# A list schedule in place of a hand-written order of the work, and another sharing of the PSUM banks

## The chip, the core and the metric

The kernel runs on one core of a Trainium2 chip. TensorE (PE) multiplies, VectorE (DVE) and ScalarE (ACT) move and transform tiles, GpSimd (POOL) builds masks and issues the DMAs that cast fp32 to bf16, SyncE (SP) issues the other DMAs. Each engine takes its instructions strictly in the order in which the program emits them; semaphores hold an instruction until its inputs are there. The metric is the device time of one execution in microseconds (us).

## The reference

For each of 4 batches the kernel computes an attention of 8 heads over 768 positions with head size 64, and feeds the result to a mixture of experts. The attention is sparse: a query sees the keys less than 16 positions away, and beside them 24 block keys (the maximum over each block of 32 keys) whose values are block means.

```python
scores_l = scale * q @ k.T                      # kept where |i - j| < 16
scores_s = scale * q @ k_blockmax.T + log(32)   # 24 block keys
a = softmax(concat([masked scores_l, scores_s]))
x = a @ concat([v, v_blockmean])                # 4 x 768 x (8*64 = 512)
e = argmax(x.mean(axis=1) @ w_gate)             # one expert of 8 per batch
out = gate_prob * (relu(x @ w1[e]) @ w2[e])     # 512 -> 1024 -> 512
```

The expert of a batch is known only when the whole attention of that batch is done; only then can its two weight matrices (2 MB each in fp32) be fetched.

## The kernel before, in words

A batch b has an attention part and an expert part (MoE). The attention part works on four pairs of heads (pr 0 to 3), each in two halves of the sequence (hf 0 and 1), with these steps:

- T(pr): TensorE transposes K into the PSUM tile kps (line 229) and Q into tps (250); K is evacuated into windows of 96 keys (244 on ScalarE in batch 0, 246 on VectorE later), Q on VectorE (256), the block maxima are taken (260) and copied beside the windows (266).
- QK(pr, hf): 12 small matmuls into sc (280), exponential (289), mask (290).
- AV(pr, hf): 12 small matmuls into one PSUM bank (316), reciprocal and scaling (324, 325).
- X(pr): transposes back (337), evacuated into xT with the sum for the gate (342).

The values of a batch are loaded in 8 DMAs, one per head, on SP's queue (`load_v`, 97). They are cast to bf16 (`cast_v`, 186 on VectorE, 184 on ScalarE), the 16 rows before and behind each block are copied by DMA (`halo_v`, 191 and 192), the block means are made on TensorE (`vsum`, 200), evacuated (209) and spread by DMA (213). `load_qk` (92) issues the loads of K and Q from POOL's queue. `gate` (395 to 441) forms the logits, finds the expert, issues the loads of w1 and w2 on POOL's queue (417, 422) and makes the scale of the output. The MoE part (`moe_groups`) has 16 groups h (451, evacuated at 458) and 6 groups o (465, evacuated at 473, stored from SP's queue at 474).

The order is written by hand. Batch 0's attention runs first, as a list of steps (line 379). From then on the MoE groups of batch b and the steps of batch b+1's attention (line 386) alternate in proportion to their number (lines 516 to 526); `LEAD` steps of batch 1 come ahead. Within a step the instructions are emitted together.

The eight PSUM banks: kps 1, tps 1, sc 2, ops 1 (AV of batches 1 to 3), mps 3 (MoE groups, the block means, the gate, and AV of batch 0).

Of the kernel before, what the change touches and what calls it, by code (L numbers as in the profile page):

```python
# [18 lines left out]
AX = mybir.AxisListType  # L19


@with_exitstack
def kernel(
# [10 lines left out]
    nc = tc.nc  # L34
# [28 lines left out]
    xt_pool = ctx.enter_context(tc.tile_pool(name="xt", bufs=2))  # L63
# [33 lines left out]
    def load_v(b):  # L97
        for h in range(H):
            if b > 0:
                nc.sync.dma_start(  # L100
                    v_f[16:80, :, h, :], v[b, h].rearrange("(j p) d -> p j d", p=QB)
                )
                continue
            j0 = 1 if h == 0 else 0
            nc.sync.dma_start(
                v_f[:, j0:NJ, h, :],
                bass.AP(
                    tensor=v.tensor,
                    offset=v.offset + (h * S + j0 * QB - 16) * D,
                    ap=[[D, 80], [QB * D, NJ - j0], [1, D]],  # L110
                ),
            )
            if h == 0:
                nc.sync.dma_start(v_f[16:80, 0, 0, :], v[0, 0, 0:QB, :])

    load_qk(0, 0, 2)
    nc.vector.memset(v_f[0:16, 0, 0, :], 0.0)
    load_v(0)
    wg_sb = const_pool.tile([128, NDT, E], FP32, name="wg_sb")
    nc.sync.dma_start(wg_sb, moe_w_gate.rearrange("(g p) e -> p g e", p=128))  # L120

    warm = const_pool.tile([1, 8], FP32, name="warm")
    nc.vector.memset(warm, 0.0)
    nc.scalar.activation(warm, warm, ACT.Exp)
    nc.vector.memset(kps.rearrange("p g c -> p (g c)").bitcast(FP32), 0.0)

    identb = const_pool.tile([128, 128], BF16, name="identb")
    make_identity(nc, identb)

# [3 lines left out]
    bind = const_pool.tile([80, NJ, 32], BF16, name="bind")  # L133
    nc.vector.memset(mask1, 1.0)
# [3 lines left out]
    def keep(t, pattern, base, mult):  # L138
# [10 lines left out]
    keep(mask1, [[-1, G], [-G, QB // G]], -1, 1)  # L149
    keep(mask1, [[1, G], [G, QB // G]], 31, -1)  # L150
    keep(row_in, [[0, 1]], 79, -1)
    keep(bind, [[QB, NJ], [-BLK, 32]], -16, 1)
    keep(bind, [[-QB, NJ], [BLK, 32]], 47, -1)
    keep(bind, [[0, NJ], [0, 32]], -16, 1)

    tok = const_pool.tile([80, 2], BF16, name="tok")
    nc.gpsimd.tensor_copy(tok[:, 0:1], v_f[:, NJ - 1, 3, 0:1])
    load_qk(0, 2, 4)
    nc.gpsimd.tensor_copy(tok[:, 1:2], v_f[:, NJ - 1, 6, 0:1])
    load_qk(0, 4, 6)  # L160
    load_qk(0, 6, 8)

    nc.vector.tensor_copy(mask[0:KW], mask1.unsqueeze(1).to_broadcast([KW, NJ, QB]))
    nc.vector.memset(mask[0:16, 0, :], 0.0)
    nc.vector.tensor_scalar(
        out=mask[0:KW, NJ - 1, :], in0=mask1, scalar1=row_in[:, 0:1], scalar2=None, op0=ALU.mult
    )
    nc.vector.memset(mask[KW:NR], 1.0)
    ones_row = const_pool.tile([1, 128], FP32, name="ones_row")
    nc.vector.memset(ones_row, 1.0)  # L170

    def init_vblk(i):
        nc.vector.memset(vblks[i][64:KW, NJ - 1, :, :], 0.0)
        nc.vector.memset(vblks[i][0:KW, :, :, D : D + 1], 1.0)

    init_vblk(0)
    for t in kts:
        nc.gpsimd.memset(t[:, :, NR:128], 0.0)

    def cast_v(b, h0, h1, eng):  # L180
        dst = vblks[b % 2][0:80, :, h0:h1, 0:D]
        src = v_f[:, :, h0:h1, :]
        if eng is nc.scalar:
            nc.scalar.activation(dst, src, ACT.Copy)
        else:
            eng.tensor_copy(dst, src)  # L186

    def halo_v(b, h0, h1):
        vb = vblks[b % 2]
        if b > 0:  # L190
            nc.sync.dma_start(vb[0:16, 1:NJ, h0:h1, :], vb[64:80, 0 : NJ - 1, h0:h1, :])
        nc.sync.dma_start(vb[80:96, 0 : NJ - 1, h0:h1, :], vb[16:32, 1:NJ, h0:h1, :])

    def vsum(b, groups):
        vb = vblks[b % 2]
        vs_ps = mps_pool.tile([128, 512], FP32, name="hps", tag="mps")
        HW = H // 2
        for j in range(NJ):
            for i, hg in enumerate(groups):
                nc.tensor.matmul(  # L200
                    vs_ps[32 * i : 32 * i + 32, 0 : HW * (D + 1)],
                    lhsT=bind[:, j, :],
                    rhs=vb[0:80, j, hg * HW : (hg + 1) * HW, :],
                    start=(j == 0),
                    stop=(j == NJ - 1),
                )
        n = 32 * len(groups)
        vsb = sm_pool.tile([64, HW, D + 1], BF16, name="vsb")
        nc.vector.tensor_copy(
            vsb[0:n], vs_ps[0:n, 0 : HW * (D + 1)].rearrange("p (h c) -> p h c", c=D + 1)  # L210
        )
        for i, hg in enumerate(groups):
            nc.sync.dma_start(
                vb[KW:NR, :, hg * HW : (hg + 1) * HW, :],
                vsb[32 * i : 32 * i + NB].unsqueeze(1).to_broadcast([NB, NJ, HW, D + 1]),
            )

    def attn_steps(b):
        q_nat, k_nat = qk_nat[b]
        vb = vblks[b % 2]  # L220
        xT = xt_pool.tile([128, NP, S], BF16, name="xT_b")
# [136 lines left out]
        def halo():  # L358
            if nxt < B:
                halo_v(nxt, 0, H)  # L360
# [196 lines left out]
```

## Time and profile before

| | us |
|---|---|
| median of 3 runs (lowest, highest) | 258.3 (257.16, 259.15) |
| the profiled execution | 257.47 |
| its span, from the first to the last instruction | 255.9 |
| PE busy in the span | 160.2 |
| DVE busy | 99.1 |
| ACT busy | 97.2 |
| POOL busy | 25.5 |

A busy share is a mean over stretches that have different limits: an engine with 63% can be the limit in one stretch and starved in another. So the span is read in stretches, and in each the wait is looked for that ended last.

### The profile page before, as it was taken

The numbers are of one execution on the slowest core, as the hardware profiler recorded it, in microseconds if no ns is written. First come the engines' busy times: TensorE is split into PE (matmuls) and PEld (weight loads), VectorE is DVE, ScalarE is ACT, GpSimd is POOL, SyncE is SP. The second block draws the span as 40 slices with busy tenths as digits, with TensorE's granted clock in tenths as the row PEclk, the third lists the DMA queues.
The fourth block names the chain that finished last, engine by engine and source line by source line (L and its number), as shares of the span: only waits on it lengthen the run. The fifth ranks groups of instructions, "written<-read, shape, count | busy, mean of one in ns | idle before, by whom it ended". The sixth has DMA issues, their size and how long they took to land. (4 is left out here: it accounts for less than half of the span.)

```text
span 255.9 us, 4606 instructions
## 1 busy us (share of the span) xinstructions
PE 160.2 (63%) x1936; PEld 95.8 (37%) x1960; DVE 99.1 (39%) x201; ACT 97.2 (38%) x183; POOL 25.5 (10%) x46
## 2 busy tenths in 40 slices
PE   0205457731254889967550498964989897539993
PEld 0203346510143655544230355442555454115541
DVE  4204337753047785237450255524464623100000
ACT  2211546620013449632300567532348555105542
POOL 7260000009000000005000000002000000200000
PEclk9999999999999999999795599999599999657998
DMA  7999209708999980469999400446950023495033
GB/s 119 191 185 179 44 14 167 108 1 124 181 207 208 208 125 4 98 148 180 198 196 204 152 3 3 106 138 103 218 120 3 0 85 124 69 207 96 0 123 123
DMA packets 46869, 30.45 MB, mean 119 GB/s; under 512 B 28224, under 2 KB 42144, under 8 KB 46752
## 3 DMA queue, kind: packets, MB, share of 16 engines
q0 software_dynamic: 13264, 14.68, 35.9%
q1 hardware_dynamic: 33584, 15.47, 29.8%
q8 instruction: 15, 0.25, 0.4%
q14 instruction: 6, 0.05, 0.1%
HBM read 36.06 MB, written 6.29 MB: 166 GB/s over the span
## 5 line engine op out<-in xcount | busy, mean ns | idle before, releaser
L451 PE MATMUL hps<-xT_b,w_sb 128*128 128x256 bf16 (+1 forms) x245 | 51.8, 348 | 22.6 <-ACT o_sb L473 12.6
L465 PE MATMUL hps<-w_sb,hT_sb 128*128 128x512 bf16 x179 | 46.5, 404 | 1.9 <-issue 1.2
L290 DVE TENSOR_TENSOR aT<-aT,mask 120x768 bf16<-120x768 bf16 x32 | 17.8, 558 | 64.5 <-ACT aT L289 64.4
L451 PEld LDWEIGHTS <-w_sb 128*128 128x128 bf16 x256 | 24.2, 104 | 39.5 <-issue 20.9
L458 ACT ACTIVATE hT_sb<-hps 128x512 bf16<-128x512 f32 x64 | 29.3, 497 | 16.8 <-PE hps L451 16.8
L473 ACT ACTIVATE o_sb<-hps,gcol 128x512 f32<-128x512 f32 x24 | 16.5, 686 | 44.2 <-PE hps L465 19.4
L289 ACT ACTIVATE aT<-sc 128x768 bf16<-128x768 f32 x32 | 25.9, 810 | 12.7 <-PE sc L280 12.7
L280 PE MATMUL sc<-qT,kT 64*128 64x64 bf16 x384 | 13.5, 212 | 25.3 <-ACT kT L266 9.4
L266 ACT ACTIVATE kT<-kmx 128x288 bf16<-128x288 bf16 x16 | 7.1, 442 | 56.3 <-DVE kmx L260 56.3
L465 PEld LDWEIGHTS <-hT_sb 128*128 128x128 bf16 x192 | 18.7, 102 | 22.0 <-issue 4.8
L200 PE MATMUL hps<-vblk,bind 80*32 80x260 bf16 x96 | 12.0, 347 | 18.1 <-DMA vblk<-vblk 9.0
L417 POOL DMA_DIRECT2D w_sb<-in_moe_w_dram x5 | 4.5, 911 | 186.7 <-DVE gcol L441 98.9
L280 PEld LDWEIGHTS <-kT 64*128 64x128 bf16 x384 | 9.7, 107 | 33.9 <-issue 14.3
L246 DVE COPY kT<-kps 128x1152 bf16<-128x1152 bf16 x12 | 16.2, 1352 | 4.1 <-PE kps L229 4.1
L200 PEld LDWEIGHTS <-bind 80*32 80x32 bf16 x96 | 7.6, 118 | 21.7 <-issue 18.5
L342 ACT ACTIVATE xT_b<-tps 128x768 bf16<-128x768 bf16 x16 | 13.0, 811 | 6.4 <-PE tps L337 6.3
L260 DVE TENSOR_REDUCE kmx<-kT 128x24 bf16<-128x768 bf16 x16 | 15.1, 943 | 0.0
L229 PE MATMUL kps<-identb,k_nat 96*64 96x96 bf16 x256 | 11.0, 245 | 6.4 <-DMA k_nat<-in_k_dram 6.4
L316 PEld LDWEIGHTS <-aT 120*64 120x64 bf16 x384 | 10.3, 127 | 9.9 <-issue 5.3
L325 DVE TENSOR_TENSOR xs<-ops,rv 128x384 bf16<-128x384 f32 x24 | 13.4, 557 | 0.8
L186 DVE CAST vblk<-v_f 80x1536 bf16<-80x1536 f32 (+1 forms) x13 | 13.4, 1042 | 0.5 <-DMA v_f<-in_v_dram 0.5
L337 PE MATMUL tps<-identb,xs 128*128 128x128 bf16 x96 | 10.3, 247 | 4.6 <-DVE xs L325 3.2
(57 smaller groups left out, 120.7 us busy)
## 6 DMA issues: line engine op xcount, KB each, us to landing
w_sb<-in_moe_w_dram POOLq DMA_DIRECT2D x7, 1024.0 KB, 13.6
out_dram<-o_sb SPq DMA_DIRECT2D x24, 256.0 KB, 2.1
v_f<-in_v_dram SPq DMA_DIRECT2D x24, 192.0 KB, 13.0
k_nat<-in_k_dram POOLq DMA_DIRECT2D x6, 384.0 KB, 18.5
q_nat<-in_q_dram POOLq DMA_DIRECT2D x6, 384.0 KB, 20.6
v_f<-in_v_dram SPq DMA_DIRECT2D x7, 240.0 KB, 7.8
vblk<-vsb SPq DMA_DIRECT2D x8, 146.2 KB
vblk<-vblk SPq DMA_DIRECT2D x6, 178.8 KB
```

Source lines behind the costliest of these rows:

```text
L186: eng.tensor_copy(dst, src)
L200: nc.tensor.matmul(vs_ps[32 * i : 32 * i + 32, 0 : HW * (D + 1)], lhsT=bind[:, j, :], rhs=vb[0:80, j, hg * HW : (hg + 1) * HW, :], start=( ...
L246: nc.vector.tensor_copy(kdst, win)
L260: nc.vector.tensor_reduce(out=kmx.rearrange("p (j n) -> p j n", n=2), in_=kT[:, :, 16:80].rearrange("p j (n w) -> p j n w", w=BLK), axis=AX.X,
L280: nc.tensor.matmul(sc[:, hh, jj * QB : (jj + 1) * QB], lhsT=kTs[pr][rs, j, :], rhs=qTs[pr][rs, j, :], start=True, stop=True, tile_position ...
L289: nc.scalar.activation(aT, sc[:, :, 0 : NH * QB], ACT.Exp, scale=SCALE)
L290: nc.vector.tensor_tensor(out=aT[0:NR], in0=aT[0:NR], in1=mask[:, hf * NH : (hf + 1) * NH, :] .rearrange("p j c -> p (j c)") .unsqueeze(1) ...
L325: nc.vector.tensor_tensor(out=xss[pr][:, hf * NS : (hf + 1) * NS, :, :].rearrange("p s h d -> p h s d"), in0=ops[:, :, :, 0:D], in1=rv.uns ...
L451: nc.tensor.matmul(hps[:, 0 : c1 - c0], lhsT=w1_sb[:, dt, ft * 128 : (ft + 1) * 128], rhs=xT_b[:, dt, c0:c1], start=(dt == 0), stop=(dt == ...
L458: nc.scalar.activation(hT[:, ft, c0:c1], hps[:, 0 : c1 - c0], ACT.Relu)
L465: nc.tensor.matmul(o_ps, lhsT=hT[:, ft, st * 128 : (st + 1) * 128], rhs=w2_sb[:, ft, :], start=(ft == 0), stop=(ft == NFT - 1),)
L473: nc.scalar.activation(o_sb, o_ps, ACT.Copy, scale=gcol[:, 0:1])
```

## The change

The emission order is no longer written out. Each step is cut into its parts (one TensorE group, one evacuation, one DMA issue), and each part is entered as an operation with its engine, a duration, its dependencies and, for a DMA, a transfer time. A list scheduler goes through the graph when the program is built: at each turn it takes the engine that can start first, and on it the operation with the longest remaining chain, or a shorter one that fits ahead of it; it emits that operation. The result is again one fixed order per engine.

```diff
+class Sched:
+    SEM = 0.06
+    URGENT = 3.0
...
+    def slot(self, tag, bufs):
+        q = self.tags.setdefault(tag, [])
+        q.append({"first": None, "readers": []})
+        deps = []
+        if len(q) > bufs:
+            deps += q[-1 - bufs]["readers"]
+        if len(q) > 1:
+            deps.append(q[-2]["first"])
+        return q[-1], deps
...
+    def run(self, t0):
...
+            tail[op["n"]] = op["dur"] + op["lat"] + (op["dma"] and op["dma"] + 2.0) + max(
+                [tail[u["n"]] for u in users.get(op["n"], [])], default=0.0
+            )
...
+                for r, op in sorted(rs, key=lambda x: x[1]["key"]):
+                    start = max(t0e, r)
+                    if pick is None:
+                        pick = (start, op)
+                    elif (
+                        start + op["dur"] <= pick[0] + 0.1
+                        or (start < pick[0] and tail[pick[1]["n"]] - tail[op["n"]] < self.URGENT)
+                    ):
+                        pick = (start, op)
...
+            if op["dma"]:
+                begin = max(rings.get(eng, 0.0), op["issued"] + 0.8)
+                other = max([f for e, f in rings.items() if e != eng], default=0.0)
+                shared = min(op["dma"], max(0.0, other - begin))
+                rings[eng] = begin + op["dma"] + shared
+                op["end"] = rings[eng] + 1.2
```

A slot of a buffer is given out in the order in which the operations were entered, never out of it. The operations of batch 0 carry a bonus of 40 in priority. Setup, loads and values:

```diff
-    xt_pool = ctx.enter_context(tc.tile_pool(name="xt", bufs=2))
+    xt_pool = ctx.enter_context(tc.tile_pool(name="xt", bufs=3))
-    for t in kts:
-        nc.gpsimd.memset(t[:, :, NR:128], 0.0)
+    def setup_dve():
+        for i in range(2):
+            nc.vector.memset(vblks[i][64:KW, NJ - 1, :, :], 0.0)
+            nc.vector.memset(vblks[i][0:KW, :, :, D : D + 1], 1.0)
+        for t in kts:
+            nc.vector.memset(t[:, :, NR:128], 0.0)
...
-    nc.gpsimd.tensor_copy(tok[:, 0:1], v_f[:, NJ - 1, 3, 0:1])
+    tk = add("POOL", 0.2, [v_loads[2], bind_setup], lambda: nc.gpsimd.tensor_copy(tok[:, 0:1], v_f[:, NJ - 1, 2, 0:1]))
+    qk_loads[0, 1] = add("POOL", 1.3, [tk], lambda: load_qk(0, 2, 4), dma=2.3)
...
+    def v_ops(b, loads):
...
+        for c in range(NP):
+            on_act = False
+            eng = nc.scalar if on_act else nc.vector
+            casts.append(
+                add("ACT" if on_act else "DVE", 1.45 if on_act else 0.95,
+                    [loads[2 * c + 1], dve_setup] + prev, lambda b=b, c=c, eng=eng: cast_v(b, c, eng)))
...
+            hl = add("SP", 1.2, cs, lambda b=b, hs=hs: halo_v(b, hs), dma=1.5)
+            sl, deps = sch.slot("ops", 1)
+            def vs(b=b, gs=gs, st=st):
+                ps = ops_pool.tile([128, 512], FP32, name="ops")
...
+            w = cs if b == 0 else cs + [hl]
+            o_vs = add("PE", 1.3 * len(gs), w + deps + [bind_setup], vs, lat=0.2)
+            o_ev = add("DVE", 0.42, [o_vs], ev)
+            o_bc = add("SP", 0.6 * len(gs), [o_ev], bc, dma=0.8 * len(gs))
```

Each cast now takes two heads, also in batch 0 (before: four heads, once on VectorE and once on ScalarE). Attention, gate and MoE have the same instructions as before; the AV groups of all batches, the block means and both matmuls of the gate take their turn on the single bank ops, and mps is left to the MoE groups:

```diff
-                if b == 0:
-                    ops_raw = mps_pool.tile([128, 512], FP32, name="hps", tag="mps")
-                else:
-                    ops_raw = ops_pool.tile([128, 512], FP32, name="ops")
+            os_, od = sch.slot("ops", 1)
+            o_av = add("PE", 0.35, [o_mk] + v_ready[b][pr // 2] + od, lambda: av(pr, hf), lat=0.2)
...
+    def gate(b, x_ops, w_deps):
+        sb = state[b]
+        sl, deps = sch.slot("ops", 1)
...
+        o_lg = add("PE", 0.25, x_ops + deps, lgf, lat=0.2)
+        o_mx = add("DVE", 0.7, [o_lg], mxf)
+        o_ld = add("POOL", 1.5, [o_mx] + w_deps, ldf)
...
+            w1a = w1b = add("POOL", 0.8, [o_ld], lambda: w1f(0), dma=5.6)
+        w2 = add("POOL", 0.8, [], w2f, dma=6.3, after=[w1b])
...
+            o = add("PE", 4 * n * 0.000422, [w1a if ft < NFT // 2 else w1b] + deps, mm_keep, lat=0.25)
+            r = add("ACT", 0.6 if n > 256 else 0.39, [o] + hdeps, rl)
...
+            o = add("PE", 1.73, need + [w2] + deps, mm, lat=0.25)
+            r = add("ACT", 0.7, [o, o_gc] + od, ev)
+            d = add("SP", 0.4, [r], st_out, dma=0.7)
```

The outer loop enters the batches one after the other. The first half of K and Q of the next batch is loaded behind the loads of this batch, the second half behind this batch's weights; the next batch's values are loaded behind the weights of the batch before this one:

```diff
+    for b in range(B):
+        sch.prio = 40.0 if b == 0 else 0.0
+        sequence, xsl, x_ops = attention(b)
+        nxt = b + 1
+        sch.prio = 0.0
+        if nxt < B:
+            prev = last_T.get(nxt - 2, [])
+            qk_loads[nxt, 0] = qk_loads[nxt, 1] = add(
+                "POOL", 1.3, prev, lambda n=nxt: load_qk(n, 0, 4), dma=4.7, after=order_pool)
+            vl = []
+            for h in range(H):
+                vl.append(add("SP", 0.6, casts, lambda n=nxt, h=h: load_v(n, h), dma=0.87,
+                              after=vl[-1:] + bcs + w_order))
+        sch.prio = 40.0 if b == 0 else 0.0
+        sequence()
+        w = gate(b, x_ops, moe_last.get(b - 2, []))
+        w_order = [w[2]]
+        sch.prio = 0.0
+        if nxt < B:
+            casts, bcs = v_ops(nxt, vl)
+            qk_loads[nxt, 2] = qk_loads[nxt, 3] = add(
+                "POOL", 1.3, prev, lambda n=nxt: load_qk(n, 4, 8), dma=4.7,
+                after=[w[2], qk_loads[nxt, 0]])
+            order_pool = [qk_loads[nxt, 2]]
+        moe_last[b] = moe(b, w, xsl)
+    sch.run({"PE": 0.0})
```

Before, all of K and Q of batch b+2 was loaded behind the weights of batch b, and the values of batch b+2 behind the block means of batch b+1.

## Rows read from the trace of the kernel before

**Rows 1.** The profile's first part: engine, busy us, share of the span, instructions.
```profile
PE 160.2 (63%) x1936; PEld 95.8 (37%) x1960; DVE 99.1 (39%) x201; ACT 97.2 (38%) x183; POOL 25.5 (10%) x46
```

**Rows 2.** Busy time by stretch: stretch, us; engines' busy us (instructions); PEclk, DMA share, GB/s.
```profile
57.00:86.00 29.00, 10.99 (x205) 8.81 (x207) 13.56 (x21) 3.20 (x5) 7.52 (x9) 1.00 1.14 178
86.00:131.00 45.00, 36.46 (x490) 20.93 (x497) 25.17 (x49) 21.13 (x43) 4.32 (x6) 0.96 0.81 138
131.00:143.00 12.00, 0.22 (x2) 0.04 (x1) 0.85 (x1) 0.00 (x0) 0.00 (x0) 0.65 1.14 219
143.00:174.00 31.00, 26.09 (x281) 15.02 (x287) 14.18 (x32) 18.02 (x38) 0.00 (x0) 0.92 0.25 66
174.00:219.00 45.00, 36.62 (x465) 20.45 (x471) 21.37 (x43) 22.48 (x45) 1.65 (x2) 0.92 0.41 89
219.00:228.00 9.00, 3.05 (x9) 1.13 (x10) 0.16 (x1) 0.69 (x1) 1.65 (x2) 0.55 0.83 140
228.00:256.00 28.00, 23.39 (x110) 11.72 (x112) 0.00 (x0) 11.31 (x22) 0.00 (x0) 0.87 0.37 96
```

**Rows 3.** The same view, two stretches without a long wait.
```profile
150.00:160.00 10.00, 9.30 (x125) 5.64 (x126) 6.79 (x11) 6.40 (x16) 0.00 (x0) 1.00 0.01 2
160.00:170.00 10.00, 9.43 (x96) 5.10 (x96) 4.39 (x10) 4.00 (x8) 0.00 (x0) 1.00 0.45 116
```

**Rows 4.** TensorE's waits: what waited, for what; us in total, times, longest.
```profile
PE hps L451 <- ACT o_sb L473: 12.6, 1, 12.6
...
PE hps L200 <- DMA vblk<-vblk: 9.0, 2, 8.5
PE sc L280 <- POOL kT L178: 8.4, 1, 8.4
...
PE hps L200 <- DVE vblk L186: 6.0, 3, 3.2
PE hps L451 <- DMA w_sb<-in_moe_w_dram: 6.0, 1, 6.0
...
PE hps L200 <- ACT vblk L184: 3.1, 1, 3.1
```

**Rows 5.** Instructions by time, start of the span: start, us, instruction [idle before].
```profile
16.94 0.63 POOL L92 DMA_DIRECT2D q_nat<-in_q_dram  x1
...
43.48 0.85 PE L229 MATMUL kps<-identb,k_nat 96*64 96x96 bf16 x16
```

**Rows 6.** The same view, around the first expert weights.
```profile
57.08 2.28 POOL L417 DMA_DIRECT2D w_sb<-in_moe_w_dram  x2 [37.81 <-DVE grec L435]
...
85.91 1.22 PE L451 MATMUL hps<-xT_b,w_sb 128*128 128x512 bf16 x3 [0.33 <-issue]
```

**Rows 7.** TensorE alone: a K transpose of batch 1, the block means of batch 2.
```profile
91.53 0.53 PE L229 MATMUL kps<-identb,k_nat 96*64 96x96 bf16 x16
...
107.60 1.51 PE L200 MATMUL hps<-vblk,bind 80*32 80x260 bf16 x24
```

**Rows 8.** SP's DMA issues by time: loads of v, the spreading of block means, stores.
```profile
38.78 7.98 SPq L100 DMA_DIRECT2D v_f<-in_v_dram  x8
...
109.60 1.75 SPq L213 DMA_DIRECT2D vblk<-vsb  x2
111.41 14.05 SPq L100 DMA_DIRECT2D v_f<-in_v_dram  x8
125.56 37.05 SPq L474 DMA_DIRECT2D out_dram<-o_sb  x5
```

**Rows 9.** The profile's DMA part: queues, then issues with median us to landing.
```profile
q0 software_dynamic: 13264, 14.68, 35.9%
q1 hardware_dynamic: 33584, 15.47, 29.8%
...
q_nat<-in_q_dram POOLq DMA_DIRECT2D x4, 192.0 KB, 5.9
```

**Rows 10.** The tile w_sb: us from issue to landing.
```profile
DMA to landing us min/median/max: 5.7/10.9/16.8
```

**Rows 11.** The tile k_nat: us from issue to landing.
```profile
DMA to landing us min/median/max: 3.7/11.1/22.7
```

**Rows 12.** The chain that ended last, its last work.
```profile
251.84 0.69 ACT o_sb L473
```

More of the change, by code (lines that the diff above doesn't have):

```diff
@@ L161 @@
[L161 to L174, printed above, removed]
@@ L189, in halo_v @@
+    def halo_v(b, hs):
         vb = vblks[b % 2]
         if b > 0:
-            nc.sync.dma_start(vb[0:16, 1:NJ, h0:h1, :], vb[64:80, 0 : NJ - 1, h0:h1, :])
-        nc.sync.dma_start(vb[80:96, 0 : NJ - 1, h0:h1, :], vb[16:32, 1:NJ, h0:h1, :])
-    def vsum(b, groups):
-        vb = vblks[b % 2]
[L196 to L205, printed above, removed]
-                )
[L207 to L215, printed above, removed]
-            )
@@ new lines, in add_X, with do @@
+        def add_X(pr, xs):
+            qs, qd = sch.slot("tps", 1)
+            o_tx = add("PE", 0.36, xs["n"] + qd, lambda: tx(pr), lat=0.2)
+            xs["s"]["readers"] = [o_tx]
+            o_xc = add("ACT", 1.02, [o_tx] + xdeps, lambda: xc(pr))
+            qs["first"], qs["readers"] = o_tx, [o_xc]
+            x_ops.append(o_xc)
+            if xsl["first"] is None:
+                xsl["first"] = o_xc
+        T, A, XS = {}, {}, {p: {} for p in range(NP)}
+        def do(what, pr, hf=0):
+            if what == "T":
+                T[pr] = add_T(pr)
+            elif what == "Q":
+                A[pr, hf] = add_QK(pr, hf, T[pr])
+            elif what == "A":
+                add_AV(pr, hf, A[pr, hf], XS[pr])
+            else:
+                add_X(pr, XS[pr])
@@ new lines, in sequence @@
+        def sequence():
+            do("T", 0)
+            do("Q", 0, 0)
+            do("T", 1)
+            do("Q", 0, 1)
+            for pr in range(NP):
+                do("A", pr, 0)
+                if pr + 1 < NP:
+                    do("Q", pr + 1, 0)
+                do("A", pr, 1)
+                if pr + 2 < NP:
+                    do("T", pr + 2)
+                if pr + 1 < NP:
+                    do("Q", pr + 1, 1)
+                do("X", pr)
+        return sequence, xsl, x_ops
@@ L471, in f @@
                     )
-                o_sb = o_pool.tile([128, DM], FP32, name="o_sb")
-                nc.scalar.activation(o_sb, o_ps, ACT.Copy, scale=gcol[:, 0:1])
-                nc.sync.dma_start(out[b, st * 128 : (st + 1) * 128, :], o_sb)
-            return f
-        groups = []
-        for ft in range(NFT):
-            groups.append((4, h(ft, 0, 512)))
-            groups.append((2, h(ft, 512, S)))
-        for st in range(NST):
-            groups.append((8, o(st)))
-        return groups
@@ L512, with ev @@
-    pend = []
-    start_attn(1)
-    for _ in range(LEAD):
-        queue.pop(0)()
-    per = (3 * 31 - LEAD) / 3.0
-    while moe:
-        total = sum(w for w, _ in moe)
-        done, n = 0, 0
-        for w, g in moe:
-            g()
-            done += w
-            while queue and n < per * done / total:
-                queue.pop(0)()
-                n += 1
-        moe, pend = pend, []
+            def ev():
+                ps["o"] = o_pool.tile([128, DM], FP32, name="o_sb")
+                nc.scalar.activation(ps["o"], ps["t"], ACT.Copy, scale=sb["gcol"][:, 0:1])
@@ new lines, in st_out @@
+            def st_out():
+                nc.sync.dma_start(out[b, st * 128 : (st + 1) * 128, :], ps["o"])
+            sl, deps = sch.slot("mps", 3)
+            need = [r for (f, c), r in relus.items() if c == (0 if st < 4 else 512)]
+            o = add("PE", 1.73, need + [w2] + deps, mm, lat=0.25)
+            osl, od = sch.slot("o", 3)
+            r = add("ACT", 0.7, [o, o_gc] + od, ev)
+            sl["first"], sl["readers"] = o, [r]
+            d = add("SP", 0.4, [r], st_out, dma=0.7)
```

750 lines of the change are left out of this document (467 added, 283 removed).

## The prediction

> **What bounds the kernel now.** I first read the engines' busy times: TensorE leads with 160 us of 256, VectorE and ScalarE have under 100 each [rows 1]. No engine is the bound of the whole span, so the question is where TensorE stands still. The second view is the busy time by stretch. Up to 57 us TensorE is busy for 160.2 - 136.8 = 23.4 us (136.8 is the sum of the seven stretches shown); from 57 to 86 for 11 of 29; from 131 to 143 not at all; from 219 to 228 for 3 of 9 [rows 2]. In the stretches from 143 to 219 attention and MoE run mixed, and TensorE is busy for 62.7 of 76 us, 83%; where no long wait falls, in the 20 us from 150 to 170, it reaches 94% [rows 2, 3]. The third view, TensorE's waits, says what ended the long gaps, and nearly all are matters of order: 8.4 us for a memset that stood on POOL behind loads which themselves waited for v; 6.0 and 3.1 us for casts of v that stood behind attention work; 8.5 us for a halo copy issued among the weight loads; 12.6 us for one evacuation of an output, whose buffer waited for a store queued behind the loads of v; and 6.0 us for the last batch's w1 [rows 4, 8]. So the bound is not an engine but the order in four places, and, in the mixed stretches, TensorE.
>
> **Part 1, the front, to the issue of batch 0's weights** (57.1 now [rows 6]). The three kT memsets go to VectorE, early; QK(0,0) then waits for the chain of its own pair, and up to 8.4 us go. The casts are entered per two heads with their own loads as inputs, so the two block means no longer wait behind attention work: up to 6.0 + 3.1 us. Subtracting all three gives 57.1 - 17.5 = 39.6. From the data: the last load of batch 0 is issued at 16.94, 0.63 long, and such a load lands after 5.9 us [rows 5, 9], so T(3) can start at 23.5; from the start of T(3) to the weights took 57.08 - 43.48 = 13.6 us [rows 5, 6], which gives 37.1. The lower end is 37.1, the upper 57.1 (each wait replaced by another). I take 41: near the lower end, because each wait has an earlier input to start from, with 1.4 us over 39.6 because VectorE now also has all casts. AV of batch 0 has one bank where it had three: it hides below VectorE's chain, which is the longer one here; without that cover it costs at most one evacuation per group, some 5 us, which lies within the bounds.
>
> **Part 2, from the weights to the first MoE matmul**: 85.91 - 57.08 = 28.8 us now [rows 6]. There TensorE waits for the halo copy, and MoE groups are emitted only behind eleven steps of batch 1. In the new order a MoE group follows its own inputs. Half of w1 lands after 5.7 us at best, a weight load after 16.8 at worst [rows 10]. The values of batch 1 are loaded and cast ahead of the gate, so the halo should be out of the weights' way. I take 6.5 us, bounds 5.7 and 16.8: first MoE matmul at 47.5.
>
> **Part 3, the work that is left for TensorE.** From 57 us on it is busy for 136.8 us [rows 2]. Part of that is the slow clock. A K transpose of 16 matmuls takes 0.85 us at 43 and 0.53 at 91.5 [rows 5, 7]; so the 11.0 us of 57 to 86 would take 6.9 at the fast level (the granted clock is recorded there as 1.00, but the durations say otherwise). Later, busy time times one less the granted clock gives 1.5 + 2.1 + 2.9 + 1.4 + 3.0 = 10.9 us [rows 2]. All fast, 121.8 us would remain. The clock fell behind the stretches in which TensorE stood, and those become fewer; I leave a third of the 15 us in: 127, of which 3 us are done before 47.5. At what busy share? 83% is what the hand order reached with its waits, 94% what it reached without [rows 2, 3]. I take the middle, 0.88: 124 / 0.88 = 140.9 us.
>
> **What hides the rest.** VectorE's 99 us and ScalarE's 97 lie within the same time at a share of about one half [rows 1]. The DMA queues need 35.9% + 29.8% of 255.9 = 168 us of 16 engines [rows 9]; at the share of 1.14 that the busiest stretches show [rows 2] that is 147 us, less than the sum, though not by much. One wait is new: the bank ops goes to the block means of batch b+1 only behind the gate of batch b, where those of batches 2 and 3 ran ahead of it. Behind the means (1.5 us) stand an evacuation and the spreading (1.75 us to issue, some 3 to land) [rows 7, 8]: about 6 us per batch in which no AV of the next batch can start. QK steps, T steps and MoE groups can run on TensorE in them, so I cost it at nothing; without that cover it is 3 x 6 = 18 us. The second half of K and Q stands on POOL's queue behind the weights and lands up to 22.7 us behind its issue [rows 11]; MoE groups cover it if the order puts them ahead of T(2). On POOL the read of the chosen expert now waits also for the MoE part two batches back (its weights' buffer); behind it in the queue stand two weight loads and the K and Q loads of two half batches, and T(2) of the next batch waits for them. At the sum's pace that MoE part is long done by then, so it costs nothing; if MoE fell behind it would cost as much as MoE is late.
>
> **The sum.** 41 + 6.5 + 140.9 = 188.4 for the last matmul; from there to the end of the span it takes what it takes now, the last evacuation at 251.84 [rows 12] and the store behind it, 255.9 - 251.8 = 4.1: 192.5. Outside the span lie 257.47 - 255.9 = 1.6 us, and the median of the runs is 0.8 above the profiled execution: **195 us**. With 83% it becomes 204, with 94% and no slow clock 181; a front at 45 adds 4. The case's own range is 181 to 208.
>
> **Rivals.**
> *Stores behind loads of v.* The loads of v stay on SP's queue with the stores, and now start only once the weights of the batch before are issued, so they always share the engines with POOL's loads. Eight of them took 7.98 us alone and 14.05 beside POOL's loads, and the stores behind those froze TensorE for 12.6 us [rows 4, 8]. Batch 3's loads of v will meet batch 0's stores. One such freeze, with the slow clock behind it (2.1 us), gives 195 + 14.7 = 210. For it: nothing in the change takes stores off that queue. Against: the scheduler stretches two queues that overlap, and may emit stores first. The Trainium skill (DMA: Bandwidth & Descriptors, Queues, rings and completion order) says that each DMA engine goes round-robin between the queues packet by packet. By that rule the queue with small packets (15.47 MB in 33584 against 14.68 in 13264 [rows 9]) gets 461 of every 1568 bytes; an estimate from this is that 7.98 us become 27, so the freeze would double and the time would be 222. The trace, 14.05, speaks for less.
>
> *TensorE's order blocks itself: slower.* The order is fixed from modelled landing times. If T(2) of batch b+1 is emitted ahead of MoE groups and its K and Q land late behind the weights, TensorE stands for up to the longest landing, 22.7 us [rows 11], three times, and starts each time at the slow clock (3.0 us, as in the last stretch [rows 2]): 195 + 3 x 25.7 = 272. It decides from an idle time of (258 - 195) / 3 = 21 us per batch on. Against it: the first half is loaded long before, which leaves TensorE work in that time.
>
> *Only the front gains.* Behind the gate of batch 0 DMA or the new wait on ops keeps the gates as far apart as now: 258 - 16 = 242.
>
> *The order is not what binds*: the engines wait for the same transfers in any order, 258. The stretch at 94% speaks against it.
>
> **Chances.** My forecast (181 to 208) 0.59; below 181 0.07; stores behind loads (208 to 225) 0.20; only the front 0.06; no change 0.03; TensorE blocked, slower 0.05. The range 178 to 220 holds about 0.8 of that. A measurement of this kernel can tell about 1% from no change; faster 0.92, same 0.03, slower 0.05.
>
> **What would show it.** In the profile after: weights of batch 0 issued near 41 (front right), the first L451 matmul of old within 7 us of it, no TensorE wait over 5 us before the last batch's weights, and a last stretch in which MoE of batch 2 covers the loads of batch 3. The forecast is wrong if gates stand 50 us or more apart, if TensorE waits for K or Q of pairs 2 and 3, or if an output's evacuation again waits for a store.

## The result, and the profile after

| | before | after |
|---|---|---|
| median of the runs (lowest, highest), us | 257.86 (257.16, 259.15) | 230.09 (229.69, 233.03) |
| the profiled execution, us | 257.47 | 229.69 |
| its span, us | 255.9 | 228.1 |

The ratio is 0.894, with an interval of 0.886 to 0.903. The kernel is 28 us faster, but 35 us slower than the forecast of 195 us, and 10 us above the range of 178 to 220.

The engines' work has hardly changed. This is the first part of the profile after, to be read against [rows 1]:

```profile
PE 163.5 (72%) x1938; PEld 97.3 (43%) x1960; DVE 100.9 (44%) x207; ACT 96.9 (42%) x182; POOL 24.6 (11%) x43
```

So the gain comes out of TensorE's idle time, 95.7 us before and 64.6 now, and what is missing lies there too. The busy time by stretch of the kernel after shows where it stands still. The columns are those of [rows 2], and the stretches are cut at TensorE's long gaps:

```profile
0.00:43.35 43.35, 24.60 (x410) 19.02 (x410) 28.35 (x67) 17.49 (x28) 10.51 (x24) 1.00 0.94 149
43.35:52.35 9.00, 5.39 (x81) 3.97 (x83) 6.31 (x10) 2.51 (x4) 5.09 (x7) 1.00 0.97 146
52.35:68.50 16.15, 13.70 (x153) 7.30 (x155) 3.38 (x8) 6.86 (x14) 0.00 (x0) 1.00 1.19 192
68.50:76.60 8.10, 0.01 (x2) 0.01 (x3) 3.91 (x6) 0.60 (x1) 0.00 (x0) 0.56 1.22 181
76.60:104.60 28.00, 26.54 (x354) 16.02 (x357) 19.45 (x37) 15.93 (x30) 4.34 (x6) 0.82 0.44 86
104.60:108.70 4.10, 0.00 (x0) 0.00 (x0) 0.00 (x0) 0.69 (x1) 0.00 (x0) 0.79 1.18 204
108.70:119.40 10.70, 10.40 (x113) 5.69 (x116) 2.26 (x6) 3.71 (x8) 0.00 (x0) 0.76 1.22 198
119.40:128.00 8.60, 0.01 (x1) 0.11 (x1) 3.89 (x6) 0.60 (x1) 0.00 (x0) 0.77 1.02 196
128.00:156.70 28.70, 26.94 (x318) 15.81 (x321) 16.67 (x32) 14.60 (x30) 3.01 (x4) 0.89 0.46 100
156.70:160.00 3.30, 0.00 (x1) 0.00 (x0) 0.56 (x1) 1.39 (x2) 0.00 (x0) 1.00 1.19 221
160.00:193.30 33.30, 32.19 (x400) 17.59 (x406) 15.96 (x36) 20.70 (x41) 1.64 (x2) 0.95 0.44 96
193.30:200.20 6.90, 0.07 (x1) 0.00 (x0) 0.16 (x1) 0.54 (x1) 0.00 (x0) 0.68 1.10 251
200.20:228.10 27.90, 23.63 (x110) 11.79 (x112) 0.00 (x0) 11.32 (x22) 0.00 (x0) 0.87 0.35 91
```

Between these gaps TensorE is busy for 94 to 97% of the time (26.54 of 28.00, 26.94 of 28.70, 32.19 of 33.30). From 52 us to the last weights it loses most of its time in four gaps, of 8.1, 4.1, 8.6 and 3.3 us, and in all four the DMA share is above 1. TensorE's waits in the kernel after name what ended each (us in total, times, longest; the fourth line belongs to the front):

```profile
PE kps L406 <- DVE kT L425: 18.0, 4, 8.6
PE hps L725 <- DMA w_sb<-in_moe_w_dram: 12.6, 3, 6.9
PE kps L406 <- DMA k_nat<-in_k_dram: 7.2, 1, 7.2
PE ops L355 <- DVE vblk L295: 5.1, 2, 3.1
PE ops L496 <- DMA vblk<-vsb: 4.1, 1, 4.1
```

Of the long waits of [rows 4] the memset's, the halo copy's and the evacuation's are gone; the block means still wait for casts, 5.1 us instead of 9.1, and the last batch's w1 for 6.9 instead of 6.0. (The 7.2 us for k_nat is the very first load of the kernel, not one of the late halves; before, that one took 6.4 us.) The first line is new: a K transpose waits for VectorE to empty the one bank kps. TensorE around the first weights and that wait, by time, as in [rows 5]:

```profile
52.35 1.49 PE L725 MATMUL hps<-xT_b,w_sb 128*128 128x512 bf16 x3 [2.32 <-DMA w_sb<-in_moe_w_dram]
...
65.31 0.53 PE L406 MATMUL kps<-identb,k_nat 96*64 96x96 bf16 x16
...
67.43 1.04 PE L725 MATMUL hps<-xT_b,w_sb 128*128 128x512 bf16 x4
76.59 0.85 PE L406 MATMUL kps<-identb,k_nat 96*64 96x96 bf16 x16 [8.12 <-DVE kT L425]
```

The first K transpose ended near 66, so why was it not evacuated until 75? VectorE in the same time:

```profile
62.53 0.56 DVE L510 TENSOR_TENSOR xs<-ops,rv 128x384 bf16<-128x384 f32 x1
71.81 0.96 DVE L295 CAST vblk<-v_f 80x1536 bf16<-80x1536 f32 x1 [8.72 <-DMA v_f<-in_v_dram]
...
74.31 0.96 DVE L295 CAST vblk<-v_f 80x1536 bf16<-80x1536 f32 x1 [0.85 <-DMA v_f<-in_v_dram]
75.19 1.35 DVE L425 COPY kT<-kps 128x1152 bf16<-128x1152 bf16 x1
...
121.58 0.96 DVE L295 CAST vblk<-v_f 80x1536 bf16<-80x1536 f32 x1 [7.75 <-DMA v_f<-in_v_dram]
...
125.72 0.96 DVE L295 CAST vblk<-v_f 80x1536 bf16<-80x1536 f32 x1 [2.49 <-DMA v_f<-in_v_dram]
126.60 1.35 DVE L425 COPY kT<-kps 128x1152 bf16<-128x1152 bf16 x1
```

VectorE stands at a cast of the next batch's values, because they have not landed, and soon after at a second one. The evacuation of K, which had its input at 66, stands behind both in VectorE's fixed order and ran at 75.19. The same picture comes one batch later at 121. What the casts wait for stands in SP's issues by time, to be held against [rows 8]:

```profile
23.23 11.51 SPq L211 DMA_DIRECT2D v_f<-in_v_dram  x8
...
51.89 22.19 SPq L211 DMA_DIRECT2D v_f<-in_v_dram  x8
...
100.09 25.39 SPq L211 DMA_DIRECT2D v_f<-in_v_dram  x8
```

The length of such a row runs from the first issue to the end of the last. Before, the eight loads of a batch took 7.98 us alone and 14.05 where they met POOL's loads [rows 8]. There was a third row, of batch 2's values behind the first weights, which the prediction didn't use:

```profile
73.92 17.63 SPq L100 DMA_DIRECT2D v_f<-in_v_dram  x8
```

Now the eight take 22 to 25 us for batches 2 and 3. The model in the scheduler gave one load 0.87 us, and up to that much again where the other queue is at work: at most 14 us of transfer for the eight. So it placed the casts where the values would have landed by its account. The expert choices of batches 0 to 3, by POOL's issue of w1:

```profile
43.35 1.50 POOL L664 DMA_DIRECT2D w_sb<-in_moe_w_dram  x2 [22.81 <-DVE grec L684]
...
95.35 0.76 POOL L664 DMA_DIRECT2D w_sb<-in_moe_w_dram  x1 [46.91 <-DVE grec L684]
...
146.77 0.76 POOL L664 DMA_DIRECT2D w_sb<-in_moe_w_dram  x1 [47.07 <-DVE grec L684]
...
189.88 0.76 POOL L664 DMA_DIRECT2D w_sb<-in_moe_w_dram  x1 [40.10 <-PE hps L759]
```

They stand 52.0, 51.4 and 43.1 us apart; in the last interval no values are loaded. Before, they stood 57.5, 59.5 and 45.4 us apart (issues at 57.08, 114.58, 174.10 and 219.50). So of the 28 us that were won 13.7 lie in the front and 15.9 between the first gate and the last; behind the last gate the kernel became 1.8 us longer.

### The profile page after: what moved, and what is told of

The parts are those of the page before. It is cut to its first block, busy times and chain, and to the rows that moved or that the text cites. A ratio compares the mean times of both kernels' runs of the same rounds, so it can differ in the third digit from the quotient of the medians.

```text
span 228.1 us, 4604 instructions
## 1 busy us (share of the span) xinstructions
PE 163.5 (72%) x1938; PEld 97.3 (43%) x1960; DVE 100.9 (44%) x207; ACT 96.9 (42%) x182; POOL 24.6 (11%) x43
## 4 chain that ended last, share of the span: by engine, by line
PE 36%; DMA 28%; SPq 15%; DVE 10%; ACT 5%; issue 3%; POOL 1%; POOLq 1%; ACTq 0%; DVEq 0%
DMA v_f<-in_v_dram 15%; PE hps L725 11%; DMA q_nat<-in_q_dram 9%; SPq L211 9%; PE hps L759 8%; DMA w_sb<-in_moe_w_dram 5%; SPq L214 4%; PE ops L355 3%; PE tps L520 3%; PE tps L431 3%; DVE kT L425 3%; PE kps L406 3%; DVE vblk L295 2%; PE sc L463 2%; PE ops L496 2%
## 5 line engine op out<-in xcount | busy, mean ns | idle before, releaser
L725 PE MATMUL hps<-xT_b,w_sb 128*128 128x256 bf16 (+1 forms) x242 | 55.2, 371 | 14.3 <-DMA w_sb<-in_moe_w_dram 12.6
L740 ACT ACTIVATE hT_sb<-hps 128x512 bf16<-128x512 f32 (+1 forms) x64 | 29.8, 489 | 38.2 <-PE hps L725 36.8
L759 PE MATMUL hps<-w_sb,hT_sb 128*128 128x512 bf16 x184 | 43.2, 380 | 0.6 <-issue 0.3
L478 DVE TENSOR_TENSOR aT<-aT,mask 120x768 bf16<-120x768 bf16 x32 | 17.7, 556 | 23.0 <-ACT aT L474 22.9
L295 DVE CAST vblk<-v_f 80x1536 bf16<-80x1536 f32 x16 | 15.2, 956 | 26.4 <-DMA v_f<-in_v_dram 26.4
L759 PEld LDWEIGHTS <-hT_sb 128*128 128x128 bf16 x192 | 17.8, 98 | 19.8 <-issue 0.2
L406 PEld LDWEIGHTS <-k_nat 96*64 96x64 bf16 x256 | 9.4, 139 | 28.0 <-issue 20.6
L496 PE MATMUL ops<-vblk,aT 120*64 120x65 bf16 x384 | 14.4, 220 | 7.2 <-DMA vblk<-vsb 4.1
L510 DVE TENSOR_TENSOR xs<-ops,rv 128x384 bf16<-128x384 f32 x32 | 17.8, 557 | 1.1
L355 PE MATMUL ops<-vblk,bind 80*32 80x260 bf16 x96 | 11.3, 348 | 5.1 <-DVE vblk L295 5.1
L509 DVE RECIPROCAL rv<-ops 128x6 f32<-128x6 f32 x32 | 6.1, 191 | 15.7 <-PE ops L496 15.6
```

Source lines behind the costliest of these rows:

```text
L295: eng.tensor_copy(dst, v_f[:, :, hs, :])
L355: nc.tensor.matmul(ps[32 * i : 32 * i + 32, 0 : HW * (D + 1)], lhsT=bind[:, j, :], rhs=vblks[b % 2][0:80, j, hg * HW : (hg + 1) * HW, :], ...
L406: nc.tensor.transpose(kps[hh * D : (hh + 1) * D, g, 2 : 2 + SP], qk_nat[b][1][:, 2 * pr + hh, g, :], identb[0:SP, 0:SP],)
L496: nc.tensor.matmul(ops[(j % 2) * QB : (j % 2 + 1) * QB, hh, jj // 2, :], lhsT=aT[0:NR, hh, jj * QB : (jj + 1) * QB], rhs=vb[0:NR, j, 2 * p ...
L510: nc.vector.tensor_tensor(out=sb["xs"][pr][:, hf * NS : (hf + 1) * NS, :, :].rearrange("p s h d -> p h s d"), in0=ops[:, :, :, 0:D], in1=r ...
L725: nc.tensor.matmul(sb["hps"][:, 0 : c1 - c0], lhsT=sb["w1"][:, dt, ft * 128 : (ft + 1) * 128], rhs=sb["xT"][:, dt, c0:c1], start=(dt == 0) ...
```

## The experiments

**The theories.** A: a cast of v waits on VectorE in front of K's evacuation, because the schedule was made with too short a time for the loads of v; the order, not the transfer, costs the time. The rivals: the transfers are late wherever the casts stand (the loads of v beside POOL's burst of weights and K/Q); the shared bank ops; VectorE simply has too much work. Every ratio is to the kernel before on the same chip; it took 256.3 to 258.9 us there (medians on four chips), so a few us between two experiments are compared by their ratios too.

**e1: a longer load in the model.** Only the figure in the graph changes, and with it the order.

```diff
-                    add("SP", 0.6, casts, lambda n=nxt, h=h: load_v(n, h), dma=0.87, after=vl[-1:] + bcs + w_order)
+                    add("SP", 0.6, casts, lambda n=nxt, h=h: load_v(n, h), dma=1.6, after=vl[-1:] + bcs + w_order)
```

> One number of the graph changes: the transfer time that the scheduler assumes for one load of v, 0.87 us, becomes 1.6 (alone the eight loads took 11.5 us to issue, beside POOL's loads 22 and 25). The program has the same instructions, in another order. Theory A (VectorE's casts of v are emitted too early because the assumed landing is too early, and the kT evacuation and T stand behind them): VectorE's wait for v falls from 26.4 us to under 12, TensorE's wait of 18.0 us for the kT evacuation to under 6, and the time falls by 8 to 16 us, to 214 to 222. Theory B (after each gate all loads of the next batch stand in one burst, and the attention waits for the burst whatever the order): the waits move from the casts to K, Q or the block means, gates stay 48 to 52 us apart, time 226 to 232.

221.47 us (220.43 to 223.35), ratio 0.869 [0.860, 0.877]. The loads still took 22.3 and 25.2 us; TensorE's wait for K's evacuation fell from 18.0 to 9.8 us, VectorE's for v from 26.4 to 20.6. The time lies at the upper end of what A expected, but both waits fell by less (A wanted under 6 and under 12). One cast per batch still stood ahead of the evacuations. A figure alone returns a fifth of the miss by the ratios, a quarter by the medians.

**e2: the second half of K and Q entered ahead of the weights**, so that the burst behind the weights is smaller.

```diff
+            qk_loads[nxt, 2] = qk_loads[nxt, 3] = add(
+                "POOL", 1.3, prev, lambda n=nxt: load_qk(n, 4, 8), dma=4.7,
+                after=[qk_loads[nxt, 0]],
+            )
+            order_pool = [qk_loads[nxt, 2]]
             vl = []
...
-            qk_loads[nxt, 2] = qk_loads[nxt, 3] = add(
-                "POOL", 1.3, prev, lambda n=nxt: load_qk(n, 4, 8), dma=4.7,
-                after=[w[2], qk_loads[nxt, 0]],
-            )
-            order_pool = [qk_loads[nxt, 2]]
```

> The second half of K and Q of the next batch is issued behind its first half, so ahead of the weights of this batch; the assumed times stay. Theory B: the burst behind each gate shrinks by a quarter, K and Q are there when pair 2 needs them, the gates come closer by 8 to 12 us each, and the time falls to 200 to 212. Theory A: the casts of v still stand ahead of the kT evacuation; the time stays within 222 to 232.

218.13 us (217.09 to 219.73), 0.856 [0.848, 0.863]. That lies between the two ranges and fits neither theory. TensorE's wait for K's evacuation is down to 0.7 us, but the loads of v for batch 1 now met those of K and Q and took 21.7 us instead of 11.5; the casts behind them delayed batch 0's gate to 51.7, and later one cast waited for 16.0 us. It looks like the fault of A at another place; this run doesn't separate it from late transfers.

**e3: both edits of e1 and e2.**

> Both edits at once. If A and B each hold a part, the time is below that of either alone, 195 to 208. If only A holds it equals the run with the longer assumed time of v, if only B the run with K and Q early, each within 3 us.

211.16 us (205.63 to 213.69), 0.831 [0.822, 0.839]: below either edit alone, above the 195 to 208 that was expected if both A and B held a part. The four runs lie 8 us apart, and the profile is that of the fastest. Here the loads of v and POOL's burst are apart for one batch. SP's issues by time:

```profile
24.80 18.44 SPq L211 DMA_DIRECT2D v_f<-in_v_dram  x8
...
64.61 7.70 SPq L211 DMA_DIRECT2D v_f<-in_v_dram  x8
...
91.55 12.02 SPq L211 DMA_DIRECT2D v_f<-in_v_dram  x4
```

The eight at 64.61, 17 us behind the last issue of the weights and with a single load of K issued since, took 7.70 us: the same loads, a third of the time. So the company makes them long.

**e4: the loads of v for batches 2 and 3 left out** (their casts read the values of an earlier batch; all else is done).

```diff
     def load_v(b, h):
+        if b > 1:
+            return
```

> The loads of v for batches 2 and 3 are left out (the values of batch 1 are used again); all else is the kernel after the change. It shows what these loads cost in all. Theory A: VectorE's wait for v falls to that of batches 0 and 1 (under 10 us), the two TensorE waits of 8 us go, time 205 to 214. Theory B: the burst is shorter by the 2 x 1.6 MB of v, K and Q land earlier by 6 to 8 us per gate; time 208 to 216 too, but then the wait for the last K and Q remains in TensorE's or ScalarE's waits.

207.73 us (206.79 to 209.10), 0.814 [0.806, 0.821]. Apart from these loads every engine has the order of the kernel after. TensorE's wait for K's evacuation fell from 18.0 to 0.8 us, VectorE's for v from 26.4 to 6.1, and the gates stood 39.9, 41.9 and 43.7 us apart. These sixteen loads carry 22 of the 35 us (21 by the ratios). Whether through VectorE's order or through the DMA engines, this run can't say; the next one can.

**e5: the casts of batches 2 and 3 emitted behind the last K evacuations of the batch before.** Loads, queues and durations as in the kernel after.

```diff
+            last_ek[b].append(o_ek)
...
                     lambda b=b, c=c, eng=eng: cast_v(b, c, eng),
+                    after=last_ek.get(b - 1, []) if b > 1 else (),
```

> The kernel after the change with one more ordering in the graph: the casts of v for batches 2 and 3 are emitted on VectorE only behind the last kT evacuation of the batch that runs; assumed times and loads as in the change. Theory A (the cast that waits for v stands ahead of the kT evacuation): TensorE's 18.0 us of waiting for the kT evacuation go to under 2, VectorE's wait for v falls below 12, and the time falls by at least as much as with the longer assumed time (221.5 there, which left one cast ahead), to 212 to 221. Theory B (the burst of loads): gates stay over 46 us apart because K and Q of pairs 2 and 3 come late; time not under 215.

210.12 us (209.02 to 211.97), 0.818 [0.811, 0.825], 2 us below A's range. The gates stood 42.5, 42.5 and 44.4 us apart, where B expected over 46. SP's issues of the values show that the transfers are no shorter:

```profile
52.14 22.73 SPq L211 DMA_DIRECT2D v_f<-in_v_dram  x8
...
90.27 25.77 SPq L211 DMA_DIRECT2D v_f<-in_v_dram  x8
```

VectorE by time shows two K evacuations ahead of the cast, which by then finds its values:

```profile
65.86 1.36 DVE L428 COPY kT<-kps 128x1152 bf16<-128x1152 bf16 x1 [1.52 <-PE kps L409]
...
69.39 1.36 DVE L428 COPY kT<-kps 128x1152 bf16<-128x1152 bf16 x1
...
73.01 0.95 DVE L295 CAST vblk<-v_f 80x1536 bf16<-80x1536 f32 x1
```

The waits of TensorE for K's evacuation and of VectorE for values, 18.0 and 26.4 us in the kernel after, are now these (the 6.8 us are all in batch 0):

```profile
PE kps L409 <- DVE kT L428: 0.7, 1, 0.7
DVE vblk L295 <- DMA v_f<-in_v_dram: 6.8, 4, 3.0
```

And TensorE's stretches from the first MoE matmul to the last batch's gap, and on to the end:

```profile
52.50:178.30 125.80, 107.37 (x1337) 60.84 (x1356) 66.19 (x130) 64.44 (x127) 8.99 (x12) 0.93 0.84 148
178.30:210.30 32.00, 22.15 (x109) 11.32 (x112) 0.16 (x1) 11.89 (x23) 0.00 (x0) 0.89 0.51 127
```

One constraint on the order returns 20 of the 35 us while v takes as long as in the kernel after. This shows A: nearly all of what e4 gained by leaving the loads out (22 us) comes back with the loads in, and the two long stops are gone. For the first of them the place of the casts is the only difference: up to the cast at 71.81 in the kernel after every engine's order is the same in both, and on TensorE the first group that stands elsewhere comes at 79.86 in e5. Behind it the list schedule moved some other operations too, so the 20 us as a whole are those of the constraint and what followed from it. That the transfers as such cost the time falls for these 20 us.

**e12: the casts of batches 2 and 3 on ScalarE.** If VectorE has too much work, this relieves it; if an engine that waits is the matter, the wait moves along.

```diff
-            on_act = False
+            on_act = b > 1
```

> The kernel after the change with the casts of v for batches 2 and 3 on ScalarE (assumed 1.45 us each) and no ordering added. Theory A, an engine's queue stands behind an instruction that waits for v: the wait moves with the casts, ScalarE waits for v for 15 us or more, and TensorE then waits for ScalarE's exponentials or evacuations of X; time 222 to 234. A rival, that VectorE simply has too much work when batch 1 and 2 run and the casts add to it: without them VectorE is free, ScalarE has room, and the time falls to 210 to 218.

228.64 us (225.22 to 230.02), against 258.87 for the kernel before: as A expected (222 to 234), and hardly better than the kernel after. ScalarE's wait for the values and TensorE's for ScalarE:

```profile
ACT vblk L293 <- DMA v_f<-in_v_dram: 14.2, 3, 10.1
...
PE hps L725 <- ACT hT_sb L740: 9.1, 1, 9.1
```

The wait went with the casts (A had 15 us or more), and now MoE's evacuation stands behind it. That VectorE has too much work falls, by this run and by e5, in which VectorE does all its work.

**e7: block means, gate and batch 0's AV back on the mps banks**, with the list schedule as it is.

```diff
-            sl, deps = sch.slot("ops", 1)
+            sl, deps = sch.slot("mps", 3)
...
+            pool, name = (mps_pool, "hps") if b == 0 else (ops_pool, "ops")
```

> The list schedule with the old sharing of the PSUM banks: block means, gate and batch 0's AV take their turn on the three banks of mps with the MoE groups. If the new sharing carries part of the gain, the time rises from 230 to 235 to 245 (MoE groups wait for the block means, which are given their bank first). If the wait on the single bank costs (the 4.1 us ahead of an AV), the time falls by up to 5. Theories A and B say nothing of the banks: 226 to 234.

232.45 us (231.25 to 234.46), 0.905 [0.898, 0.912]; its interval overlaps that of the kernel after (0.886 to 0.903). The order came out otherwise as well: TensorE waits 6.4 us for K's evacuation instead of 18.0, but 6.8 us at an AV whose bank VectorE couldn't empty while it stood 8.7 us at a cast of v. As far as one run with another order can tell, the other sharing of the banks is neither the gain nor the miss.

**e8: the kernel before with the kT memsets on VectorE**, a part of the change that can be made alone.

```diff
-        nc.gpsimd.memset(t[:, :, NR:128], 0.0)
+        nc.vector.memset(t[:, :, NR:128], 0.0)
```

> The kernel before, with the hand order, and only the three kT memsets moved from POOL behind the loads to VectorE's setup. It prices the first wait of the front that the prediction took off (8.4 us). If the wait was on the path: the weights of batch 0 are issued 5 to 8 us earlier and the time falls by as much, to 250 to 253. If the casts of v behind it take its place: within 2 us of the kernel before.

250.55 us (249.60 to 252.95), 0.976 [0.968, 0.983]. Batch 0's weights were issued at 51.58 instead of 57.08 [rows 6]. By the ratio some 6 of the 28 us won are this memset, measured in the hand order; in the front, 5.5 of the 13.7 us.

**e6: e5, and the second half of K and Q early for batches 2 and 3** (the edit of e2, for these batches alone).

> The casts of v behind the last kT evacuation, as in the run with that ordering alone (210.1), and for batches 2 and 3 the second half of K and Q is issued ahead of the weights. If the loads of K and Q are still what the attention waits for (Theory B on top of A; TensorE there still waited 4.5 us for K and 5.0 for Q): 202 to 207. If A was all of it: 208 to 212.

215.68 us (214.20 to 217.59), 0.835 [0.829, 0.841]: 5.6 us slower than e5 (4.4 by the ratios), and not what I expected. The loads of v behind the first weights now took 32.14 us, and on VectorE the K evacuations went first, but the second cast still stopped everything behind it:

```profile
68.86 1.36 DVE L428 COPY kT<-kps 128x1152 bf16<-128x1152 bf16 x1
...
72.48 0.95 DVE L295 CAST vblk<-v_f 80x1536 bf16<-80x1536 f32 x1
...
82.15 0.96 DVE L295 CAST vblk<-v_f 80x1536 bf16<-80x1536 f32 x1 [7.55 <-DMA v_f<-in_v_dram]
```

**e14 and e13: the casts later still, behind the gate of the batch before**; e14 with the loads of the kernel after, e13 with the K and Q loads of e6.

```diff
+        o_mx = gate_mx[b] = add("DVE", 0.7, [o_lg], mxf)
...
+                    after=[gate_mx[b - 1]] if b > 1 else (),
```

> Casts of v for batches 2 and 3 are emitted behind the read of the previous batch's gate (the maximum on VectorE) and not only behind its K evacuations. Theory A (the cast blocks VectorE only while K evacuations stand behind it): 207 to 213 us, as with the cast behind the K evacuations (210.1); no wait of a cast over 3 us. Rival (block means and the halo of the next batch now come late and hold its AV): over 214, with a TensorE wait of the block means or AV for v over 6 us per batch.

> The same cast order, and the second half of K and Q of batches 2 and 3 loaded early, ahead of the weights. With the casts only behind the K evacuations this early load gave 215.7 instead of 210.1, and VectorE's casts waited 16.9 us for v. Theory A (those casts still stood ahead of other work of VectorE while v took 32 us): with the casts behind the gate the loss goes, 202 to 210 us, the casts' wait falls below 6 us and TensorE no longer waits for K halves. Rival (the early K and Q lengthen the loads of v and of the weights, wherever the casts stand): 213 to 219.

e14 took 217.25 us (216.63 to 220.78), 0.841 [0.834, 0.848]; e13 215.75 (214.76 to 217.15), 0.837 [0.831, 0.843]. Both miss what A expected. In e14 TensorE's matmuls of the block means waited for the halo copies twice (3.0 and 3.2 us), which is most of the 7 us over e5 (6 by the ratios), although no cast waited for more than 2.7 us; so the rival had the time right, with half the wait that it named. In e13 the longest wait of a cast was 2.8 us, against 7.5 in e6, and the time is that of e6: the loads of v took 32.08 us there too. That fits the rival: with K and Q early the lateness of the transfers sets the time, and A explains only the casts placed too early. It is argued from these two runs, not shown by one that shortens the loads. Late weights may have a part as well: TensorE waits 16.9 us for them in e6 and 9.6 in e13, where e5 has 7.8. My reason for e2 was also a misreading: the one wait for k_nat in the kernel after is its first load. In e5 there is a second one, of 4.5 us at 150, before batch 3's late half; e6 and e13 no longer have it and lose more than that elsewhere.

**e11: e5 with w1 of the last batch fetched in two halves**, as batch 0's already is; e9, e10 and e15 are the same edit on e6, e3 and e13.

```diff
-            fs = slice(half * (F // 2), (half + 1) * (F // 2)) if b == 0 else slice(0, F)
+            fs = slice(half * (F // 2), (half + 1) * (F // 2)) if b in (0, B - 1) else slice(0, F)
```

> The ordering of the casts alone, and w1 of the last batch in two halves. TensorE's 5.5 us wait ahead of the last MoE becomes 2 to 3: 207 to 208. If the loads of w1 share the engines evenly, so that two halves land no earlier than one whole: 210.

> As the run with the ordering and K and Q of batches 2 and 3 early, and w1 of the last batch in two halves. If the wait for w1 in the last stretch is on the path: 2 to 3 us less than that run. If the last MoE is held by w2 or its own work: equal to it.

> K and Q ahead of the weights and the longer assumed time of v, as in the run with both, and besides w1 of the last batch is loaded in two halves, so that its first groups can start behind the first half. In the run with both TensorE stood 7.0 us before the last batch's MoE. If that wait is the landing of w1: it becomes 3 to 4 us and the time is 206 to 209. If the DMA engines or MoE's own work set the end: 210 to 213.

> As the run before it, with w1 of the last batch fetched in two halves, which gave 3.6 us (210.1 to 206.5) and 3.3 us (215.7 to 212.4) in two pairs so far: 2.5 to 4 us below that run. If the last weights are no longer what TensorE waits for: the same time.

e11: **206.51 us** (205.50 to 207.48), 0.801 [0.796, 0.806], the best of all and 10% under the kernel after. e9: 212.42 (210.05 to 215.13); e10: 208.54 (208.00 to 212.34); e15: 211.39 (211.20 to 211.88). The pairs on e5, e6 and e13 differ by 3.6, 3.3 and 4.4 us. The pair on e3 differs by 2.6, which says little: e3's fastest run, 205.63, lies below all of e10's. In e11 the last wait for w1 is 2.85 us, where e5 has 5.51 and the kernel after 6.90.

## Why the prediction was wrong

- **Part 1, the front**: 41 forecast, 43.35 measured. The mechanism was right: the memset's wait is gone (e8 shows it alone). The size was off by what the sum took off whole, 9.1 us for casts: the block means still wait 5.1 us for them.
- **Part 2, to the first MoE matmul**: 6.5 forecast, 9.0 measured, within the bounds of 5.7 and 16.8; TensorE waited 2.32 us for the first half of w1, 9.0 us behind its issue, where the best row had 5.7.
- **Part 3 is the step that failed**: the busy share of 0.88, "the middle" of 83% and 94%, and with it a third of the slow clock. From the first MoE matmul (52.35) to the last (224.1) it took 171.7 us instead of 140.9. TensorE was busy for 133.5 of them instead of 124, and idle for 38.2 instead of 16.9. The share is 0.78. The 83% was that of 143 to 219 us alone; over the like part, from 86 us to the last matmul at 251.8, the hand order had 125.8 / 165.8 = 0.76, so the share of the whole hardly moved. The idle time holds 8.1 + 8.6 us behind the casts, 4.1 for the new wait on ops, 10.3 for weights (3.4 and 6.9). The busy time holds the slow clock: one less the granted clock, times the busy time, over the stretches above, is 4.8 + 2.5 + 3.0 + 1.6 + 3.1 = 15.0 us, as much as before, where I left 5.
- Both ends of that share came from stretches of the old order, in which no cast stood ahead of its values for long (VectorE waited 0.5 us for v in the whole kernel before). They bounded nothing about the new one, and the step had no term for an engine that stands at a late transfer with other engines' work behind it. VectorE's 99 us at "a share of about one half" were no cover either: an engine with time to spare still holds up what is queued behind the instruction it waits at.
- **e5 gives the size**: with the casts out of the way its share is (107.37 + 22.15) / 153.8 = 0.84 and its profiled execution 211.97, so of the 35.6 us by which the profiled execution of the kernel after (229.7) misses the forecast for it (194.1), 17.7 are this order in that pair, and 20 by the medians. Of the 15 us that remain, the front and Part 2 hold about 5 and the last w1, by e11, about 4. The slow clock of e5, worked out as above from its two stretches, is 7.5 + 2.4 = 9.9 us, 5 more than I left in. The rest is small waits and wasn't taken apart.
- **The rival "stores behind loads of v"** had the right transfer and the wrong victim: the outputs' evacuations waited for stores for 6.2 us in all, 2.3 at most. For the length I preferred 14.05, the row of a batch in which the eight loads began at 111.41, 3 us ahead of the weights (issued at 114.58), and passed over the 17.63 at 73.92 in the same trace. The Trainium skill (DMA: Bandwidth & Descriptors, Queues, rings and completion order) has the DMA engines go round-robin between queues packet by packet. The prediction's estimate from that, with the profile's mean packets of the whole kernel, was 27 us; the runs show 22.2 and 25.4 in the kernel after, 18.2 and 27.1 in e7 with the same loads beside them, and 32 with more of K and Q (e6, e13). So in the kernel after they are nearer to the rule's estimate than to 14.05. What 230 us needed, late values in front of VectorE's other work, is in none of the rivals, and none of their sums gives that time.
- **The new wait on ops**, priced at nothing, cost 4.1 us once (AV behind the spreading of the block means), and in e7 the old sharing wins nothing. The spreading, put at some 3 us to land, let AV start 8.7 us behind its issue there. **TensorE's order blocks itself** did not come by late K or Q: it waited 1.6 us for q_nat and, behind the start, not at all for k_nat. But the signs that I had named for a wrong forecast did come, gates 52.0 and 51.4 us apart.
- **The drain** was right: the last evacuation begins at 224.09, 4.0 us before the end.

## What to carry to other kernels

A static list schedule is no better than its transfer times: an operation that waits for a DMA should not be emitted ahead of work that has its inputs and that another engine needs, and a landing time measured alone is no bound for one beside other queues. When you price a change of order, look for what each in-order engine would stop at if one transfer came late, however low its busy share. And order the waiting operation just behind the work that it must not block, not as late as possible: e14 lost 6 to 7 us of what e5 had won.

## What the runs showed of the hardware

The same eight loads of v (256-byte rows) took 7.7 us with one load of K issued beside them (e3), 18 to 27 beside the weights and two half loads of K and Q, and 32 with more of K and Q (e6, e13). With the same loads beside them they took the less, the later they began behind the weights: 27.1 us at 1.6 us behind the issue of w1 (e7), 25.4 at 4.7 and 22.2 at 8.5 (the kernel after), 18.2 at 11.5 (e7). The row that I had gone by, 14.05, is less than a doubling.

A stop of TensorE costs more than its length. In the kernel after the granted clock was 0.50 around the end of the 8.1 us stop, the lower of the two levels (1.2 and 2.4 GHz), and a K transpose took 0.85 us where it had taken 0.53 before the stop. Over the 28 us behind that stop the slow clock cost 4.8 us by the working above. Two short stretches of that kernel, 72 to 76 us and the one behind it:

```profile
72.00:76.00 4.00, 0.00 (x0) 0.00 (x0) 3.12 (x5) 0.00 (x0) 0.00 (x0) 0.50 1.25 166
76.00:80.00 4.00, 3.28 (x44) 2.56 (x45) 3.97 (x5) 1.51 (x4) 0.00 (x0) 0.50 0.30 35
```

With fewer stops e5's mean clock is 0.943 in the profiled execution, against 0.892; over all runs it is 0.906 to 0.967, against 0.892 to 0.918, so single runs overlap.
